# Weight steps handed out one at a time, token tiles as the outer loop of the second product, and sums of x made earlier

## The chip, the core and the metric

The kernel runs on one core of a Trainium2 chip. The metric is the device time of one execution in microseconds (us), the median of several runs. The engines are TensorE (PE in the profile; PEld is its weight load), VectorE (DVE), ScalarE (ACT), GpSimd (POOL) and the sync engine (SP), which only issues DMAs here. Each engine works through its own queue in order and waits on semaphores for the others.

## The reference

Three layers follow each other on 2 x 576 = 1152 tokens of width 512; all inputs are float32.

```python
# 1. attention with a window of 128 and a bias that falls with distance, 8 heads of 64
scores = where(mask, scale * q @ k.T + bias, -1e9)
x = softmax(scores) @ v
# 2. four experts, mixed by given weights p (rows of domain_probs, normalised)
for e in range(4):
    h = maximum(x @ w1[e], 0)            # 512 -> 1024
    out += p[:, e:e+1] * (h @ w2[e])     # 1024 -> 512
# 3. squared relu
h = maximum(out @ w_in, 0)               # 512 -> 2048
return (h * h) @ w_out                   # 2048 -> 512
```

## The kernel before, in words

Precision: each float32 operand is split into a rounded high part and a low part (`wh` and `wl`, `xh` and `xl`, `hh` and `hl`), and each product is three matmuls: high by high, high by low, low by high. ScalarE makes the high part by a copy, VectorE or GpSimd the low part by a subtraction.

Attention, with 24 of the 32 items of expert 0 between it, is ordered by a planner (class `Plan`), which the change does not touch. What follows is written out by a loop over `items`. An item is one piece of the first product of a layer: for expert 0 and for the last layer (which counts as experts 4 and 5) it is one slice of 128 hidden units on a chunk of 256 or 384 tokens (`gemm1`, 12 matmuls). For experts 1 to 3 it is a pair: `gemm1_pair` computes 256 hidden units for two blocks of tokens (2 x 256 in chunk 0, 2 x 320 in chunk 1) by seven products of 6 matmuls each instead of eight. It does so with sums and differences of the weights (`ha`, `hs` and low parts `la`, `ls`, made by `w_forms`) and of x (`t1`, `t2`, `m4`, `t3`, made by `x_forms`; the high part is `ht`, `hm` or is written into `xh` itself). In the order of the products: `p1` is ScalarE's copy of the first, `u2` VectorE's sum of the second with it, `p5` ScalarE's copy of the third; then relu of the first quarter, `u3`, `c12` with its relu, `c21` with its relu, and GpSimd's `c22` with its relu. Three PSUM banks take the seven products, and the second use of a bank waits until VectorE or ScalarE has read the first. TensorE therefore waits for `p1`, `u2`, `p5` and `u3` if they come late. The profile calls them `p`, `u` and `c`.

`pend` holds the h of one pair (or of three items of `gemm1`) back. `flush_one` then does the second product (`gemm2_pair` or `gemm2`, outputs `yacc`, one PSUM bank for each tile of 128 tokens) and, at the last slice, `evac` empties the banks into `y`. In a pair the loop over the two halves of h is the outer one and the loop over tiles the inner one, and `evac` comes after all tiles.

Weights: `loads` issues the DMA of a weight from the sync queue when a buffer is free. `w_ops` gives the list of steps that turn a loaded weight into its parts. For experts 1 to 3 that is one step for `w2` (ScalarE `wh`, 128 x 1024, then GpSimd `wl`) and ten for `w1` (ScalarE `ha`; four GpSimd sums `wsum`; two GpSimd `la`; ScalarE `hs`; GpSimd `ls`). For the last layer, whose weights come as 64-bit numbers, there are 14 steps on ScalarE and VectorE (`split64`, lines 199 to 214, with `wh` and `wl` at L326 and L328). The list `bg` holds the steps that are not yet issued. Once for each item `pace` computes a quota from the times at which the items should begin (`begins`), and `bg_some` issues half of it behind the first product and half behind the second. `want` issues what is still missing of the weight that comes next. `x_step` issues one of the six steps of `x_forms`, three times in an item that is a pair and once otherwise.

So it is the place in this loop that fixes where a step stands in the queue of its engine: behind an item's own instructions, in front of the next item's.

Of the kernel before, what the change touches and what calls it, by code (L numbers as in the profile page):

```python
# [130 lines left out]
def kernel(  # L131
# [132 lines left out]
    def w_forms(i):  # L264
# [27 lines left out]
        def done():  # L292
# [12 lines left out]
            lambda: (part_lo(4, 2, a22), free.append(buf)),  # L305
            lambda: nc.scalar.activation(out=t["hs"][0], in_=t["s"], func=ACTF.Copy),
# [573 lines left out]
    def gemm1_pair(e, ch, g):  # L880
# [36 lines left out]
        add(u2, pb, p1)  # L917
        mm(pc, s1, f["t1"], True, False)
        nc.scalar.activation(out=p5, in_=pc, func=ACTF.Copy)
        mm(pa, a12, f["b21"], False, True)  # L920
        relu(0, 0, pa)
        mm(pb, s3, f["t3"], False, False)
        add(u3, pb, p1)
        mm(pc, s4, f["b22"], False, True)
        add(c12, pc, u2)
        relu(0, 1, c12)
        mm(pb, a22, f["m4"], False, True)
# [3 lines left out]
        relu(1, 1, c22)  # L931
        return h

    def gemm2_pair(e, ch, g, h, tiles, first, last):
        (wh, _), (wl, _) = w2t[e, g]
        for fo, (hh, hl) in enumerate(h):
            for i, y in tiles:
                ns = slice(i * P, (i + 1) * P)
                for j, (l_, r_) in enumerate(((hh, wh), (hh, wl), (hl, wh))):
                    nc.tensor.matmul(  # L940
                        out=y, lhsT=l_[:, ns], rhs=r_[:, fo, :],
                        start=(first and fo == 0 and j == 0),
                        stop=(last and fo == FTQ - 1 and j == 2),
                    )
# [110 lines left out]
    def flush_one():  # L1055
# [8 lines left out]
        if paired(e):  # L1064
            gemm2_pair(e, ch, f, h, ys[e, ch], first, last)
        else:
            gemm2(e, ch, f, h, ys[e, ch])
        w_done(w2t, e, ch, f)
        if last:
            tiles = ys.pop((e, ch))  # L1070
            evac(e, ch, tiles)
            if e == E - 1 and f == NQ - 1:
                x2todo.extend(PAIRS[ch][0] // P + i for i, _ in tiles)
# [36 lines left out]

    def closures(i):
        e, _, k = order[i]
        return 14 if e >= E else 10 if paired(e) and k == 0 else 1

    def pace(it):
# [3 lines left out]
        for i in range(wnext["ops"], min(wnext["ops"] + 12, len(order))):  # L1119
            n += closures(i)  # L1120
            most = max(most, n / max(begins[item_of(i)] - 6.0 - now, step))
        return -int(-most * step // 1)
# [199 lines left out]
    xbg = x_forms(0, "DVE") + [[]] * 2 + x_forms(1, "DVE")  # L1322
# [20 lines left out]
    for it, (e, ch, f) in list(enumerate(items))[N1:]:  # L1343
# [7 lines left out]
        quota = pace(it)  # L1351
# [18 lines left out]
        x_step()  # L1370
# [50 lines left out]
```

## Time and profile before

| | us |
|---|---|
| median of 3 runs | 710.21 |
| the runs | 708.23, 710.21, 710.31 |
| profiled execution | 708.31 |
| its span, first to last instruction | 706.5 |
| TensorE matmul busy | 677.6 (96%) |
| VectorE busy | 413.3 (58%) |
| ScalarE busy | 298.6 (42%) |
| GpSimd busy | 295.9 (42%) |

The busy share of TensorE is that of records whose ends are modelled, so it does not say that the array is at its peak; it says where TensorE had nothing to run. [...] Times in rows are counted from the start of the span. Attention and the planner's items end at about 153, expert 0 at about 185, experts 1 to 3 at about 497, and the last layer takes the rest.

### The profile page before, as it was taken

Reading aid. Unit: us, or ns where it says so; the run is one execution under the profiler, and the core shown is the slowest. Engines: PE = TensorE matmul, PEld = TensorE weight load, DVE = VectorE, ACT = ScalarE, POOL = GpSimd, SP = SyncE. Lnnn points to the kernel's source line nnn. Section 1 sums busy time; section 2 is a strip of 40 time slices with the busy share of each in tenths; the row PEclk is TensorE's granted clock in tenths of the full one; section 3 lists DMA queues with packets and bytes.
Section 4 is the critical chain, followed back from the end, with each engine's and each line's share of the span. In section 5 each row is a group of like instructions: output and inputs, shape, how many; then the busy total and the mean of one; then the engine's idle time right before and its main releaser. Section 6 shows DMA issues by size and latency. Waiting matters only on the chain.

```text
span 706.5 us, 10701 instructions
## 1 busy us (share of the span) xinstructions
PE 677.6 (96%) x3992; PEld 610.4 (86%) x3992; DVE 413.3 (58%) x880; ACT 298.6 (42%) x700; POOL 295.9 (42%) x314
## 2 busy tenths in 40 slices
PE   8789999999969999999998999989989999999997
PEld 7689999899957989898988999887979999989996
DVE  4778787639287454445442546876886676542121
ACT  5977676624133342333333234333445444432221
POOL 4998656535243664734836351000222223222221
PEclk7989999999979999999999999999999999999999
DMA  8752221003101100101101102216520120001011
GB/s 216 221 145 79 73 79 51 10 31 120 59 31 57 63 31 31 60 32 59 60 31 61 60 0 90 90 60 221 196 61 0 60 90 30 2 1 45 1 45 45
DMA packets 37108, 47.63 MB, mean 67 GB/s; under 512 B 3392, under 2 KB 25408, under 8 KB 37056
## 3 DMA queue, kind: packets, MB, share of 16 engines
q1 hardware_dynamic: 37056, 46.95, 20.9%
q8 instruction: 31, 0.51, 0.3%
q14 instruction: 21, 0.17, 0.1%
HBM read 44.58 MB, written 2.36 MB: 66 GB/s over the span
## 4 chain that ended last, share of the span: by engine, by line
PE 87%; DVE 6%; ACT 2%; POOL 2%; issue 1%; SPq 1%; DMA 1%; ACTq 0%; POOLq 0%
PE yacc L940 20%; PE yacc L971 20%; PE hps L810 20%; PE hps L891 18%; PE xps L631 4%; PE tp L733 2%; PE sc L685 2%; DVE fxwork L846 1%; DVE wl L328 1%; DMA wraw<-in_w_dram 1%; SPq L1164 1%; POOL wl L402 1%; DVE wroom L214 1%; ACT wh L326 0%; PE xps L613 0%
## 5 line engine op out<-in xcount | busy, mean ns | idle before, releaser
L971 PE MATMUL yacc<-wh,hmem 128*128 128x512 f32 x432 | 147.5, 394 | 0.0
L940 PE MATMUL yacc<-wh,hmem 128*128 128x512 f32 x432 | 137.1, 390 | 0.0
L961 POOL TENSOR_TENSOR hmem<-r,hmem 128x384 fp32r<-128x384 f32 x48 | 52.1, 1085 | 167.2 <-ACT hmem L960 167.2
L810 PE MATMUL hps<-xh,wh 128*128 128x384 f32 (+1 forms) x320 | 104.0, 325 | 1.6 <-ACT wh L326 1.3
L810 PE MATMUL hps<-xh,wl 128*128 128x384 f32 (+1 forms) x320 | 102.8, 321 | 0.6 <-DVE wl L328 0.6
L810 PE MATMUL hps<-xl,wh 128*128 128x384 f32 (+1 forms) x320 | 102.3, 320 | 0.0
L940 PEld LDWEIGHTS yacc<-wh,hmem 128*128 128x128 f32 x432 | 81.1, 188 | 16.4
L971 PEld LDWEIGHTS yacc<-wh,hmem 128*128 128x128 f32 x432 | 81.2, 188 | 15.3
L971 PE MATMUL yacc<-wl,hmem 128*128 128x512 f32 x216 | 85.1, 394 | 0.0
L940 PE MATMUL yacc<-wl,hmem 128*128 128x512 f32 x216 | 84.3, 390 | 0.0
L930 POOL TENSOR_TENSOR c<-u,p 128x256 f32<-128x256 f32 (+1 forms) x24 | 19.5, 814 | 144.3 <-DVE u L901 144.3
L959 DVE TENSOR_TENSOR r<-hps,r 128x384 f32<-128x384 f32 x48 | 26.7, 556 | 79.0 <-ACT r L958 79.0
L810 PEld LDWEIGHTS hps<-xh,wh 128*128 128x128 f32 x320 | 60.3, 189 | 4.9 <-ACT wh L326 1.7
L810 PEld LDWEIGHTS hps<-xl,wh 128*128 128x128 f32 x320 | 60.3, 188 | 2.3
L958 ACT ACTIVATE r<-hps 128x384 f32<-128x384 f32 x48 | 23.5, 490 | 90.0 <-PE hps L810 90.0
L810 PEld LDWEIGHTS hps<-xh,wl 128*128 128x128 f32 x320 | 60.2, 188 | 1.2 <-DVE wl L328 1.2
L905 ACT ACTIVATE hmem<-c 128x256 fp32r<-128x256 f32 (+1 forms) x72 | 29.4, 439 | 74.1 <-DVE c L901 74.1
L906 DVE SCALAR_TENSOR_TENSOR hmem<-c,hmem 128x256 fp32r<-128x256 f32 (+1 forms) x72 | 45.7, 661 | 24.5 <-ACT hmem L905 24.5
L901 DVE TENSOR_TENSOR u<-hps,p 128x256 f32<-128x256 f32 (+1 forms) x48 | 21.8, 455 | 58.0 <-PE hps L891 49.2
L721 POOL TENSOR_SCALAR ts<-ts,st 128x256 f32<-128x256 f32 (+2 forms) x80 | 38.4, 495 | 28.1 <-DVE st L716 14.4
L940 PEld LDWEIGHTS yacc<-wl,hmem 128*128 128x128 f32 x216 | 40.6, 188 | 7.7
L971 PEld LDWEIGHTS yacc<-wl,hmem 128*128 128x128 f32 x216 | 40.6, 188 | 6.5
(130 smaller groups left out, 1550.3 us busy)
## 6 DMA issues: line engine op xcount, KB each, us to landing
wraw<-in_w_dram SPq DMA_DIRECT2D x32, 512.0 KB, 3.5
wraw<-in_w_in_dram SPq DMA_DIRECT2D x16, 512.0 KB, 4.3
wraw<-in_w_out_dram SPq DMA_DIRECT2D x16, 512.0 KB, 3.6
rq<-in_qT_dram SPq DMA_DIRECT2D x8, 256.0 KB, 5.9
out_dram<-y SPq DMA_DIRECT2D x8, 256.0 KB, 2.1
rk<-in_kT_dram SPq DMA_DIRECT2D x8, 192.0 KB, 3.5
rv<-in_v_dram SPq DMA_DIRECT2D x8, 192.0 KB, 2.9
rq<-in_qT_dram SPq DMA_DIRECT2D x8, 192.0 KB, 2.5
```

The costliest lines, as they stand in the source:

```text
L631: nc.tensor.matmul(out=xps[0:rows, o0:o0 + w], lhsT=l_, rhs=r_, start=start, stop=(i == len(mm) - 1 and a == 0 and l_ is wl_), skip_group_ ...
L721: nc.gpsimd.tensor_scalar(out=ts[0:n, g, :], in0=ts[0:n, g, :], scalar1=st[0:n, 2, g:g + 1], scalar2=1.0, op0=ALU.mult, op1=ALU.mult,)
L810: nc.tensor.matmul(out=ps, lhsT=l_[:, k, cs], rhs=r_[:, k, cols], start=(k == 0 and r_ is xh and l_ is wh and not second), stop=(k == KT - ...
L891: nc.tensor.matmul(out=ps, lhsT=a[l_][:, k, :], rhs=b[r_][:, k, :], start=start and k == 0 and l_ == r_, stop=stop and k == 1 and l_ == 1, ...
L901: nc.vector.tensor_tensor(out=out, in0=x, in1=y, op=ALU.add)
L905: nc.scalar.activation(out=hh, in_=src, func=ACTF.Relu)
L906: nc.vector.scalar_tensor_tensor(out=hl, in0=src, scalar=0.0, in1=f32(hh), op0=ALU.max, op1=ALU.subtract)
L940: nc.tensor.matmul(out=y, lhsT=l_[:, ns], rhs=r_[:, fo, :], start=(first and fo == 0 and j == 0), stop=(last and fo == FTQ - 1 and j == 2),)
L958: nc.scalar.activation(out=r, in_=ps, func=ACTF.Relu)
L959: nc.vector.tensor_tensor(out=r, in0=ps, in1=r, op=ALU.mult)
L961: nc.gpsimd.tensor_tensor(out=hl, in0=r, in1=f32(hh), op=ALU.subtract)
L971: nc.tensor.matmul(out=y, lhsT=l_[:, ns], rhs=r_[:, fo, :], start=(f == 0 and j == 0), stop=(f == FT - 1 and j == 2),)
```

## The change

1. `fill(share)` is new. It adds a share of the item's quota to an account and issues a step for each whole one. `gemm1_pair` calls it behind five of its seven products, and `flush_one` behind each tile of a second product. The two calls of `bg_some` for each item are gone. `pace` returns a number that is not rounded, and it wants the weights of a pair 12 us ahead instead of 6.
2. The list of steps of `w_forms` gets two empty steps ahead of `hs`.
3. `gemm2_pair` does one tile for both halves of h before the next one, and `evac` of a tile follows that tile.
4. The steps of `x_forms` for chunk 1 follow those of chunk 0 without a gap, two in an item, so that they are all issued within expert 0, the last two behind its last item.
5. `loads` is called a second time in each item.

```diff
--- before.py
+++ after.py
@@ -303,6 +303,8 @@
             lambda: add(6, lambda: a12, s(2), ALU.subtract),
             lambda: part_lo(0, 4, raw[:, :, 0:P]),
             lambda: (part_lo(4, 2, a22), free.append(buf)),
+            lambda: None,
+            lambda: None,
             lambda: nc.scalar.activation(out=t["hs"][0], in_=t["s"], func=ACTF.Copy),
             done,
         ]
@@ -915,33 +917,38 @@
         nc.scalar.activation(out=p1, in_=pa, func=ACTF.Copy)
         mm(pb, s2, f["t2"], True, False)
         add(u2, pb, p1)
+        fill(0.6)
         mm(pc, s1, f["t1"], True, False)
         nc.scalar.activation(out=p5, in_=pc, func=ACTF.Copy)
+        fill(0.6)
         mm(pa, a12, f["b21"], False, True)
         relu(0, 0, pa)
         mm(pb, s3, f["t3"], False, False)
         add(u3, pb, p1)
+        fill(0.6)
         mm(pc, s4, f["b22"], False, True)
         add(c12, pc, u2)
         relu(0, 1, c12)
+        fill(0.6)
         mm(pb, a22, f["m4"], False, True)
         add(c21, pb, p1)
         relu(1, 0, c21)
         nc.gpsimd.tensor_tensor(out=c22, in0=u3, in1=p5, op=ALU.add)
         relu(1, 1, c22)
+        fill(0.6)
         return h
 
-    def gemm2_pair(e, ch, g, h, tiles, first, last):
+    def gemm2_pair(e, ch, g, h, tile_, first, last):
         (wh, _), (wl, _) = w2t[e, g]
+        i, y = tile_
+        ns = slice(i * P, (i + 1) * P)
         for fo, (hh, hl) in enumerate(h):
-            for i, y in tiles:
-                ns = slice(i * P, (i + 1) * P)
-                for j, (l_, r_) in enumerate(((hh, wh), (hh, wl), (hl, wh))):
-                    nc.tensor.matmul(
-                        out=y, lhsT=l_[:, ns], rhs=r_[:, fo, :],
-                        start=(first and fo == 0 and j == 0),
-                        stop=(last and fo == FTQ - 1 and j == 2),
-                    )
+            for j, (l_, r_) in enumerate(((hh, wh), (hh, wl), (hl, wh))):
+                nc.tensor.matmul(
+                    out=y, lhsT=l_[:, ns], rhs=r_[:, fo, :],
+                    start=(first and fo == 0 and j == 0),
+                    stop=(last and fo == FTQ - 1 and j == 2),
+                )
 
     def gemm1(e, ch, f):
         n = chunks(e)[ch][1]
@@ -1061,14 +1068,17 @@
         if first:
             n = 2 * PAIRS[ch][1] if paired(e) else chunks(e)[ch][1]
             ys[e, ch] = [(i, ps_tile("y", [P, DM], "yacc")) for i in range(n // P)]
-        if paired(e):
-            gemm2_pair(e, ch, f, h, ys[e, ch], first, last)
-        else:
-            gemm2(e, ch, f, h, ys[e, ch])
+        for tile_ in ys[e, ch]:
+            if paired(e):
+                gemm2_pair(e, ch, f, h, tile_, first, last)
+            else:
+                gemm2(e, ch, f, h, [tile_])
+            if last:
+                evac(e, ch, [tile_])
+            fill(1.0)
         w_done(w2t, e, ch, f)
         if last:
             tiles = ys.pop((e, ch))
-            evac(e, ch, tiles)
             if e == E - 1 and f == NQ - 1:
                 x2todo.extend(PAIRS[ch][0] // P + i for i, _ in tiles)
 
@@ -1108,18 +1118,29 @@
                 w_start()
             bg_run(1)
 
+
+    quota = dict(n=0, per=1.0, left=0.0)
+
+    def fill(share):
+        quota["left"] += quota["n"] * share / quota["per"]
+        while quota["left"] >= 1.0:
+            quota["left"] -= 1.0
+            bg_some(1)
+
     def closures(i):
         e, _, k = order[i]
-        return 14 if e >= E else 10 if paired(e) and k == 0 else 1
+        return 14 if e >= E else 12 if paired(e) and k == 0 else 1
 
     def pace(it):
 
         n, most = len(bg), 0.0
         now, step = begins[it], begins[it + 1] - begins[it]
         for i in range(wnext["ops"], min(wnext["ops"] + 12, len(order))):
+            e = order[i][0]
             n += closures(i)
-            most = max(most, n / max(begins[item_of(i)] - 6.0 - now, step))
-        return -int(-most * step // 1)
+            early = 12.0 if paired(e) else 6.0
+            most = max(most, n / max(begins[item_of(i)] - early - now, step))
+        return most * step
 
     def w_done(parts, e, ch, f):
         if paired(e):
@@ -1319,7 +1340,7 @@
     attn_close()
     fxwork, fxbuf = zip(*(w_tile([P, 2 * PAIRS[1][1]], F32, "fxwork") for _ in range(2)))
 
-    xbg = x_forms(0, "DVE") + [[]] * 2 + x_forms(1, "DVE")
+    xbg = x_forms(0, "DVE") + x_forms(1, "DVE")
 
     def x_step():
         if xbg:
@@ -1348,7 +1369,7 @@
             want(2 * (pend[0][0] * NQ + (pend[0][2] if paired(pend[0][0]) else pend[0][2] // FTQ)) + 1)
         if it > x2wait and (it - x2wait) % 2:
             run_x2()
-        quota = pace(it)
+        quota["n"] = pace(it)
         if paired(e):
             h = gemm1_pair(e, ch, f)
             if it == items.index((E, 0, 0)) - 1:
@@ -1367,15 +1388,17 @@
                 flush_one()
         pend.append((e, ch, f, h))
         w_done(w1t, e, ch, f)
-        x_step()
+        loads()
+        for _ in range(2):
+            if e or len(xbg) > 2 or f == FT - 1:
+                x_step()
         if paired(e):
-            x_step()
-        bg_some(quota - quota // 2)
+            quota["per"] = 3.0 + 2 * PAIRS[ch][1] / P
+        else:
+            quota["per"] = 1.0 + chunks(e)[ch][1] / P
+            fill(1.0)
         if len(pend) > (1 if paired(e) else LAG):
             flush_one()
-        if paired(e):
-            x_step()
-        bg_some(quota // 2)
     while bg or carry:
         bg_run()
         while carry:
```

The order of instructions shows three places. In the names, `wraw` is a loaded weight, `fxwork` the room in which a sum of x is made, and `yacc` and `hps` are PSUM banks; a number behind a name tells apart what would read alike. The line numbers of the changed kernel differ from those of the kernel before by 2 to 7 here.

On ScalarE, from the last relu of the first pair to the second pair's copies `p`, about 191 to 207 in the profile. Before:

```order
L905 ACTIVATE hmem<-c_2542 128x256
L864 ACTIVATE ht_2636<-fxwork 128x640
L306 ACTIVATE hs<-wsum 128x1024
L326 ACTIVATE wh<-wraw 128x1024
L864 ACTIVATE ht_2642<-fxwork 128x640
L287 ACTIVATE ha<-wraw 128x512
L287 ACTIVATE ha<-wraw 128x256
L915 ACTIVATE p_2668<-hps 128x256
L919 ACTIVATE p_2669<-hps 128x256
```

The same place in the changed kernel:

```order
L907 ACTIVATE hmem<-c_2566 128x256
L287 ACTIVATE ha<-wraw 128x512
L287 ACTIVATE ha<-wraw 128x256
L308 ACTIVATE hs<-wsum 128x1024
L328 ACTIVATE wh<-wraw 128x1024
L917 ACTIVATE p_2689<-hps 128x256
L922 ACTIVATE p_2690<-hps 128x256
```

The two `ht` of chunk 1 (L864) are gone from between the pairs. `hs`, `wh` and one `ha` still stand ahead of the second pair's `p`.

On VectorE, the end of expert 0 up to the first `u` of the first pair, about 169 to 186 in the profile; L953 is the split of h of an item of expert 0. Before:

```order
L846 TENSOR_TENSOR lt_2331<-fxwork,ht_2330 128x512
L846 TENSOR_TENSOR fxwork<-xh 128x512
L846 TENSOR_TENSOR fxwork<-fxwork,xl 128x512 x2
L953 SCALAR_TENSOR_TENSOR hmem<-hps,hmem 128x384
L846 TENSOR_TENSOR lm_2361<-fxwork,hm_2360 128x512
L953 SCALAR_TENSOR_TENSOR hmem<-hps,hmem 128x384
L846 TENSOR_TENSOR xl<-fxwork,xh 128x2x256
L953 SCALAR_TENSOR_TENSOR hmem<-hps,hmem 128x384 x2
L901 TENSOR_TENSOR u_2538<-hps,p_2536 128x256
```

The same place in the changed kernel (L960 is the split):

```order
L848 TENSOR_TENSOR fxwork<-xh,fxwork 128x640
L848 TENSOR_TENSOR fxwork<-fxwork,xl 128x640
L848 TENSOR_TENSOR lt_2409<-fxwork,ht_2408 128x640
L848 TENSOR_TENSOR fxwork<-xh 128x640
L848 TENSOR_TENSOR fxwork<-fxwork,xl 128x640 x2
L960 SCALAR_TENSOR_TENSOR hmem<-hps,hmem 128x384 x3
L848 TENSOR_TENSOR lm_2446<-fxwork,hm_2445 128x640
L848 TENSOR_TENSOR xl<-fxwork,xh 128x2x320
L903 TENSOR_TENSOR u_2562<-hps,p_2560 128x256
```

The work of chunk 1 (640 columns) has moved in ahead of the last three splits of expert 0, and its last two instructions stand ahead of the first `u`.

On VectorE, from the emptying of five tiles in expert 3 to the next pair's `u`, about 441 to 450 in the profile. Before:

```order
L328 TENSOR_TENSOR wl<-wroom,wh 128x512
L214 SCALAR_TENSOR_TENSOR wroom<-wroom 128x512
L203 TENSOR_SCALAR wroom<-wraw_4783 128x512
L989 SCALAR_TENSOR_TENSOR y<-yacc,pt,y 128x512 x5
L206 TENSOR_SCALAR wroom<-wroom 128x512
L210 SCALAR_TENSOR_TENSOR wroom<-wraw_4783,wroom 128x512
L328 TENSOR_TENSOR wl<-wroom,wh 128x512
L214 SCALAR_TENSOR_TENSOR wroom<-wroom 128x512
L203 TENSOR_SCALAR wroom<-wraw_4903 128x512
L901 TENSOR_TENSOR u_4911<-hps,p_4909 128x256
```

The same place in the changed kernel:

```order
L996 SCALAR_TENSOR_TENSOR y<-yacc,pt,y 128x512
L210 SCALAR_TENSOR_TENSOR wroom<-wraw_4774,wroom 128x512
L330 TENSOR_TENSOR wl<-wroom,wh 128x512
L214 SCALAR_TENSOR_TENSOR wroom<-wroom 128x512
L996 SCALAR_TENSOR_TENSOR y<-yacc,pt,y 128x512 x2
L203 TENSOR_SCALAR wroom<-wraw_4776 128x512
L206 TENSOR_SCALAR wroom<-wroom 128x512
L996 SCALAR_TENSOR_TENSOR y<-yacc,pt,y 128x512
L210 SCALAR_TENSOR_TENSOR wroom<-wraw_4776,wroom 128x512
L330 TENSOR_TENSOR wl<-wroom,wh 128x512
L903 TENSOR_TENSOR u_4908<-hps,p_4906 128x256
```

The five emptyings (L989, now L996) no longer stand in one piece: steps of the last layer's weights stand between them, and two instead of five stand between the last of them and `u`.

## Rows read from the trace of the kernel before

**Rows 1.** Busy time by stretch: stretch; its length; PE, PEld, DVE, ACT, POOL; clock; DMA

```profile
184.70:211.20 26.50, 19.90 (x113) 17.98 (x112) 17.34 (x23) 7.73 (x16) 8.62 (x6) 0.81 0.09 32
204.00:211.20 7.20, 6.95 (x35) 6.65 (x36) 5.21 (x6) 1.08 (x3) 5.12 (x5) 0.61 0.21 73
475.70:479.30 3.60, 3.60 (x16) 3.60 (x15) 1.21 (x3) 0.47 (x1) 0.86 (x1) 0.53 0.02 5
540.00:700.00 160.00, 160.00 (x800) 144.34 (x799) 71.02 (x116) 58.31 (x113) 40.48 (x38) 1.00 0.09 30
```

**Rows 2.** Waits of TensorE: who waited for whom; us in total, times, longest

```profile
PE hps L891 <- ACT hs L306: 4.3, 1, 4.3
PE hps L891 <- ACT p L915: 3.6, 2, 1.8
PE hps L891 <- DVE u L901: 3.3, 2, 1.9
```

**Rows 3.** The chain that ended last: start, us, what

```profile
184.88 5.12 PE hps L891 x42
...
211.17 5.47 PE yacc L940 x24
...
219.57 1.04 ACT hs L306
...
220.99 3.78 PE hps L891 x24
...
265.74 6.15 PE hps L891 x42
...
466.68 0.34 DVE wroom L203
...
467.36 0.60 DVE wroom L210
```

**Rows 4.** Timeline, VectorE and ScalarE, 194 to 201: start, us, instruction, [idle before <-releaser]

```profile
194.82 2.11 DVE L985 TENSOR_SCALAR y<-yacc,pt 128x512 f32<-128x512 f32 x3 [2.69 <-PE yacc L971]
...
199.41 0.74 ACT L864 ACTIVATE ht<-fxwork 128x640 fp32r<-128x640 f32 x1 [7.76 <-DVE fxwork L846]
200.06 1.04 ACT L306 ACTIVATE hs<-wsum 128x1024 fp32r<-128x1024 f32 x1
```

**Rows 5.** Timeline around three later waits of TensorE, 386 to 476

```profile
386.28 1.06 ACT L306 ACTIVATE hs<-wsum 128x1024 fp32r<-128x1024 f32 x1 [4.78 <-POOL wsum L281]
...
387.24 1.04 ACT L326 ACTIVATE wh<-wraw 128x1024 fp32r<-128x1024 f32 x1
...
388.61 0.38 PE L891 MATMUL hps<-xh,ha 128*128 128x256 f32 x1 [1.84 <-ACT p L915]
...
443.84 3.38 DVE L989 SCALAR_TENSOR_TENSOR y<-yacc,pt,y 128x512 f32<-128x512 f32 x5
...
450.08 0.39 PE L891 MATMUL hps<-xh,hs 128*128 128x256 f32 x1 [1.42 <-DVE u L901]
...
475.06 0.41 PE L891 MATMUL hps<-xh,hs 128*128 128x320 f32 x1 [1.91 <-DVE u L901]
```

**Rows 6.** Sums of x: line L846 in one stretch, then VectorE and GpSimd beside them

```profile
156.00:184.70 28.70, 16.01 (x14) 1.00 0.30 100
...
156.25 0.56 DVE L953 SCALAR_TENSOR_TENSOR hmem<-hps,hmem 128x384 fp32r<-128x384 f32 x1 [3.23 <-ACT hmem L952]
...
163.61 0.68 DVE L846 TENSOR_TENSOR lt<-fxwork,ht 128x512 fp32r<-128x512 f32 x1
...
164.65 2.64 POOL L402 TENSOR_TENSOR ls<-wsum,hs 128x1024 fp32r<-128x1024 f32 x1 [4.44 <-ACT hs L306]
...
165.05 2.78 DVE L846 TENSOR_TENSOR fxwork<-fxwork,xl 128x512 f32<-128x512 f32 x1
...
386.20 1.97 POOL L402 TENSOR_TENSOR la<-wraw,ha 128x512 fp32r<-128x512 f32 x2
...
388.12 2.39 POOL L402 TENSOR_TENSOR ls<-wsum,hs 128x1024 fp32r<-128x1024 f32 x1
```

## The prediction

> **What bounds the kernel now.** I read the profile in this order: the granted clock and busy time by stretch, the waits of TensorE, the chain that ended last, then the timeline around each wait. [...]
>
> Undisturbed, a pair product (42 matmuls) takes 5.12 us at 256 tokens and 6.15 us at 320, so one of its seven products takes 0.73 or 0.88 us; a second product of 24 matmuls takes 5.47, or 0.228 each [rows 3].
>
> **Term A, expert 0 to expert 1.** From 184.88 to 211.17 TensorE does two pairs and 27 matmuls of `yacc` [rows 3]: 2 x 5.12 + 27 x 0.228 = 16.4 us of work in 26.3 us. The loss is 9.9 us. The cause stands in the timeline [rows 4]: VectorE empties three `y` tiles (2.11 us from 194.82) and then makes chunk 1's sums of x. ScalarE's `ht` waits 7.76 us for them, and behind it in ScalarE's queue stands `hs`, which TensorE needs. [...]
>
> The change takes these sums out of that stretch: the order of ScalarE shows no `ht` ahead of `hs` there any more. But VectorE must now do them in the items before. Its queue from the split at 156.25 [rows 6] to the last split of expert 0 holds 14 instructions of 512 columns at 0.68, 12 of 640 columns (at 0.68 x 640/512 = 0.85 by proportion, an estimate), 8 splits of 0.5 (0.56 [rows 6] less the overlap of one with the next) and 2 emptyings at 0.70 (a third of 2.11 [rows 4]): 9.5 + 10.2 + 4.0 + 1.4 = 25.1 us. To this come the times in which GpSimd holds VectorE up. The rows show the hold-up: at 165.05 a 0.68 us instruction took 2.78 us, and ended as GpSimd's `ls`, begun at 164.65 for 2.64 us, was over; the 14 instructions took 16.0 instead of 9.5 us, 6.5 more [rows 6]. Laid out in the new order, one after the other, the collisions that I find are the last weight sum (0.6), about 0.8 of the pair of `la` (1.97), 1.4 of the first `ls` (2.39 less a split that reads PSUM beside it) and all of one `wl` (the size of `ls`, 2.39): 5.2 us. VectorE also idles some 1.2 us for ScalarE's copies. That puts the last split at 156.25 + 25.1 + 5.2 + 1.2 = 187.8, and the third last, which frees the PSUM bank that the first pair begins in, about 1.0 us earlier: 186.8. TensorE wants the bank at 184.88: a wait of 1.9 us that was not there before. Bounds: no collisions give 181.6 and no wait; the 6.5 us of before, again in proportion for the 12 (5.6), give 193.7 and a wait of 8.8. I take 1.9, the layout by single rows.
>
> [...]
>
> Behind the wait two small ones follow. In the first pair `u` stands behind the last two forms (2 x 0.85), which take turns with four GpSimd sums: I get 1.3 us (bounds 0 and 3). In the second pair `p` stands behind `hs` and `wh` (1.06 and 1.04 [rows 5]), and `hs` waits for GpSimd's sums, which queue behind `ls` and `wl`: 1.5 us (bounds 0 and 3). [...] New loss 1.9 + 1.3 + 1.5 + 0.8 = 5.5; gain 9.9 - 5.5 = **4.4**.
>
> **Term B, the third pair.** `p` came late behind `hs` at 219.57 [rows 3], which waited for the last forms. The two waits for `p` sum to 3.6 us, the longest is 1.8 [rows 2]; this one is the other, 1.7, and the restart costs 3.78 - 24 x 0.146 = 0.3. With no form and no step of weights in ScalarE's queue there any more, **2.0** are gained; bounds 0 and 2.0.
>
> **Term C, the pair at 388.** `hs` waited 4.78 us for GpSimd's sums, `wh` came behind it, and `p` behind both; TensorE lost 1.84 [rows 5]. The two empty steps put `hs` later than the sums, and `fill` puts it between tiles of a second product. Gain **1.8**; bounds 0 and 2.1.
>
> **Term D, the pair at 450.** Five emptyings (3.38 us) stood in a lump with the steps ahead of `u`; TensorE lost 1.42 [rows 5]. Now each tile is emptied as it is finished, but the count of steps is the same. After the preceding pair VectorE has its tail (three instructions and the copies between them, 2.4 us by estimate), 5 x 0.68 of emptying (3.38 / 5 [rows 5]) and nine step instructions (four at 0.34 and five at 0.60 [rows 3]: 4.4): 10.2 us against 30 matmuls, 30 x 0.228 = 6.8. `u` then starts 3.4 - 0.2 us into a pair that asks for it after 4 x 0.73 = 2.9 and needs 0.4 for it: 0.6 stays. Gain **0.8**; bounds -1 and 1.4.
>
> **Term E, the pair at 475.** [...] By the reckoning of D: 2.4 + 4 x 0.68 + 2.5 = 7.6 us against 5.47, so `u` is done 2.6 us into a pair that asks for it at 4 x 0.88 = 3.5. Gain 1.9 + 1.3 = **3.2**; bounds 0 and 3.2.
>
> **Term F, steps within the pairs.** 18 of the 24 pairs now get one to seven steps between their products. Costly is the place after the third product: `p` has been copied, and ScalarE's relu of the first quarter follows, from which `h`'s low part and then `u`'s successor hang, due 1.46 (256) or 1.76 us (320) later. The chain itself needs about 1.3 or 1.65, so a ScalarE step of 1.04 there shows as some 0.3 us. In the new order such a step (`wh`, or the first of a squared-relu weight) stands there in four pairs; elsewhere it is a GpSimd step, an empty one, or stands after the critical instruction. Loss 4 x 0.25 = **1.0**; bounds 0 and, if all 18 pay 1 us, 18.
>
> **Edits at nothing.** The tile-outer order changes neither the number nor the shape of matmuls, and each tile's six follow each other as twelve already do in the first product; what hides the later release of the second weights is that they are let go once per item, as before. Earlier `loads()` moves DMAs on the sync queue ahead; no wait of TensorE's after 150 is on one. Waits of the squared-relu layer's first items (`wh` and `wl`, about 2 us) stay: the step they hang on is still given out just ahead; bounds -2 and +2. In the last 180 us nothing waits, so finer hand-outs gain nothing.
>
> **Sum.** 4.4 + 2.0 + 1.8 + 0.8 + 3.2 - 1.0 = 11.2 us. The profiled execution took 708.31 (span 706.5 and 1.8 around it): 697.1. The median of the runs shown is 710.21, 1.9 above it, the other runs at 708.23 and 710.31; I say **697.5**, a little above the sum.
>
> **Rivals.**
> 1. The forms overload VectorE: every collision counts, the first pair waits 8.8 instead of 1.9 us and the clock falls as before (2.9 instead of 0.8). For it: 16.0 us for 9.5 us of work. Against it: of the 28.7 us of that row the 14 instructions, the splits and the emptyings leave 28.7 - 16.0 - 4.0 - 1.4 = 7.3 free. Time 697.1 + 6.9 + 2.1 = 706.1. Chance 0.12.
> 2. The lumps near the last expert only change shape, since VectorE's total there is the same: D and E stay, 697.1 + 4.0 = 701.1. Chance 0.13.
> 3. The spread steps cover everything: the new waits of A and F and the rest of D vanish, 697.1 - 5.5 - 1.0 - 0.6 = 690.0. Chance 0.12.
> 4. Slower: steps within the pairs. A ScalarE step of 1.05 us with a VectorE step of up to 0.69 behind it in front of the accumulating quarter holds TensorE in each of the 18 pairs. It undoes the gain from (11.2 + 1.0) / 18 = 0.68 us a pair on; at 0.9 a pair, 697.1 - 1.0 + 16.2 = 712.3. For it: before, no pair had steps inside, and its slack is 0.1 to 0.2 us. Against it: most steps there are GpSimd's. Chance 0.08.
>
> My forecast, 693 to 702, has 0.55. The range 689.5 to 705.5 holds the forecast, rivals 2 and 3 and part of the first. A measurement of this kernel can tell about 0.3% (2.1 us) from no change. Faster than that: forecast, rivals 2 and 3 and most of 1, 0.87; slower 0.08; between them 0.05.
>
> **What would show it.** [...] The prediction is wrong if the first pair waits over 6 us, if the pairs show TensorE waiting in most of them, or if the last 180 us change.

## The result and the profile after

The changed kernel takes 700.83 us (median of 4 runs, 700.31 to 702.1) against 709.91 us: 0.9879 of the time before, with a 95% interval of 0.9857 to 0.9901. Timed once more in a later comparison it came to 0.9863 (0.9842 to 0.9885). The forecast was 697.5 with a range of 689.5 to 705.5: right in sign and range, 3.3 us too low. How far its reasons held is told term by term further down.

TensorE's waits from the trace after answer to [rows 2] (who waited for whom; us in total, times, longest):

```profile
PE hps L893 <- ACT p L917: 1.8, 1, 1.8
PE hps L893 <- DVE u L903: 1.8, 3, 0.7
PE xtp L1009 <- DVE xl L1014: 1.5, 1, 1.5
PE xtp L1009 <- DVE c L903: 1.4, 1, 1.4
...
PE hps L812 <- ACT wh L328: 1.1, 1, 1.1
PE hps L812 <- DVE wl L330: 1.0, 1, 1.0
...
PE hps L893 <- DVE hmem L960: 0.7, 1, 0.7
```

The kernel before also had these, which [rows 2] leaves out:

```profile
PE hps L891 <- POOL ls L402: 2.2, 1, 2.2
PE hps L810 <- ACT wh L326: 1.3, 1, 1.3
PE xtp L1002 <- DVE xl L1007: 1.0, 1, 1.0
PE hps L810 <- DVE wl L328: 0.6, 1, 0.6
```

The 4.3 us for `hs` and the 2.2 for `ls` are gone. The 3.6 for `p` have become one wait of 1.8, and the 3.3 for `u` three waits of at most 0.7. The transposes (`xtp`) of the last layer's input, which waited once for 1.0 us, now wait twice, 2.9 us together. The waits for `wh` and `wl` in the last layer have stayed at some 2 us.

The chain of work that ended last answers to [rows 3] (start, us, what):

```profile
182.86 2.87 POOL wl L330
...
190.85 2.48 PE hps L893 x18
193.33 6.15 PE yacc L978 x27
199.48 2.16 PE hps L893 x18
...
202.07 1.04 ACT wh L328
203.11 0.28 ACT p L917
...
203.43 4.31 PE hps L893 x24
207.74 5.81 PE yacc L947 x24
```

The 24 second-product matmuls of the first pair start at 207.74; before, they started at 211.17 [rows 3]. In front of them stands what is left of the loss: `p` came late because ScalarE still had `wh`, and `hs` ahead of that, to do. The trace shows ScalarE doing them in the order of its queue: `p` follows at 203.11, at the end of the 1.04 us of `wh`, though its matmuls were done at 201.64.

Busy time by stretch answers to [rows 1] (columns as there; the clock is the granted TensorE clock as a share of its full speed):

```profile
183.00:213.00 30.00, 26.77 (x150) 23.54 (x149) 18.05 (x26) 11.40 (x24) 25.39 (x19) 0.94 0.20 70
203.40:207.80 4.40, 4.37 (x25) 4.37 (x26) 2.02 (x5) 1.05 (x3) 4.40 (x3) 0.67 0.27 89
512.30:513.30 1.00, 0.94 (x3) 0.95 (x4) 1.00 (x4) 0.36 (x1) 0.00 (x0) 0.50 0.42 94
553.00:613.00 60.00, 60.00 (x302) 54.28 (x301) 36.70 (x60) 26.90 (x52) 16.13 (x14) 1.00 0.11 36
```

Two stretches run below full clock: 203.4 to 207.8 (0.67) and a little beyond (0.87 up to 210.0), behind the wait for `p`, and 512.3 to 515.6 (0.51), behind the waits for `wh` and `wl`. After that the squared-relu layers run as before, with no idle time: TensorE is busy for all of the 60.00 us of the last row, at 1.00.

The timeline answers to [rows 4] and [rows 5] (start, us, instruction, [idle before <-releaser]):

```profile
174.44 0.74 ACT L866 ACTIVATE ht<-fxwork 128x640 fp32r<-128x640 f32 x1 [4.89 <-DVE fxwork L848]
...
182.63 3.77 DVE L848 TENSOR_TENSOR fxwork<-fxwork,xl 128x640 f32<-128x640 f32 x2
...
201.10 1.06 ACT L308 ACTIVATE hs<-wsum 128x1024 fp32r<-128x1024 f32 x1 [1.74 <-POOL wsum L281]
...
443.54 0.39 PE L893 MATMUL hps<-xh,hs 128*128 128x256 f32 x1 [0.72 <-DVE u L903]
...
473.74 0.44 PE L1009 MATMUL xtp<-ident,y 128*128 128x128 f32 x2 [1.54 <-DVE xl L1014]
```

`ht` now waits at 174, where TensorE has other work. The two sums at 182.63 take 3.77 us where two of them alone took 0.82 each just before: GpSimd's `wl` runs from 182.86 to 185.72 beside them. That is the hold-up of [rows 6] once more.

**Where the gain stands.** I take the start of the same second product in every trace: before, 182.63, 224.61, 377.62, 391.67, 464.01, 482.57 and 530.35; after, 183.97, 219.54, 373.39, 385.34, 457.46, 474.15 and 523.39. The same +1.34 of the first stands already at 102.92 against 104.26 us, far ahead of the change, so it is a difference between executions and is taken off. Gains over before in us, stretch by stretch, for the profiled execution of each kernel below; the last three columns are their sum, and the median and ratio of the timed runs. Each ratio is to the kernel before as timed beside it (708.3 to 709.9 us), so rows are better compared by ratio than by median:

| kernel | to 225 | to 378 | to 392 | to 464 | to 483 | to 530 | sum | median | ratio (95%) |
|---|---|---|---|---|---|---|---|---|---|
| changed | 6.4 | -0.8 | 2.1 | 0.2 | 1.9 | -1.5 | 8.3 | 700.8 | 0.9879 (0.9857-0.9901) |
| changed, again (e5) | 6.5 | -0.8 | 2.1 | 0.2 | 1.5 | -2.7 | 6.8 | 700.0 | 0.9863 (0.9842-0.9885) |
| e1 early sums alone | 9.3 | 0.0 | -1.4 | 0.0 | 1.0 | 0.0 | 8.8 | 699.4 | 0.9859 (0.9841-0.9878) |
| e2 sums as before | 2.4 | -1.4 | 2.1 | -0.3 | 1.5 | -2.5 | 1.8 | 706.3 | 0.9952 (0.9935-0.9969) |
| e3 none within pairs | 3.0 | 0.0 | 2.1 | -4.1 | 1.4 | -0.8 | 1.6 | 703.2 | 0.9937 (0.9911-0.9963) |
| e4 tiles inner | 7.7 | -0.8 | 2.1 | 0.2 | 1.9 | -1.4 | 9.7 | 700.7 | 0.9873 (0.9856-0.9890) |
| e6 shares add to one | 9.9 | -0.9 | 2.1 | 0.1 | 0.9 | -3.2 | 8.9 | 700.8 | 0.9866 (0.9841-0.9892) |
| e7 + none in last pair | 10.0 | -0.9 | 2.1 | 0.1 | 3.2 | -3.5 | 11.0 | 697.3 | 0.9825 (0.9801-0.9849) |
| e8 + last weights early | 9.9 | -0.9 | 2.1 | -0.7 | 3.1 | 3.1 | 16.5 | 692.8 | 0.9762 (0.9739-0.9785) |
| e9 lumps, due early | 7.1 | 0.0 | 2.1 | -0.6 | -0.9 | 2.4 | 10.1 | 699.8 | 0.9870 (0.9852-0.9888) |
| e10 changed, last early | 6.4 | -0.8 | 2.1 | 0.0 | 2.1 | -0.1 | 9.7 | 698.6 | 0.9861 (0.9844-0.9878) |
| e11 no empty steps | 6.1 | -1.0 | 2.1 | -1.2 | 1.9 | -1.7 | 6.2 | 703.0 | 0.9915 (0.9896-0.9934) |

### The profile page after: what moved, and what is told of

It is laid out like the page before. It is cut to its first block, busy times and chain, and to the rows that moved or that the text cites. A ratio compares the mean times of both kernels' runs of the same rounds, so it can differ in the third digit from the quotient of the medians.

```text
span 699.5 us, 10689 instructions
## 1 busy us (share of the span) xinstructions
PE 678.3 (97%) x3992; PEld 611.6 (87%) x3992; DVE 412.2 (59%) x880; ACT 297.7 (43%) x700; POOL 294.8 (42%) x314
## 4 chain that ended last, share of the span: by engine, by line
PE 84%; DVE 8%; ACT 3%; issue 2%; POOL 1%; DMA 1%; SPq 1%; ACTq 0%; DVEq 0%; POOLq 0%
PE yacc L947 20%; PE hps L812 19%; PE yacc L978 19%; PE hps L893 17%; PE xps L633 4%; PE tp L735 2%; PE sc L687 2%; DVE fxwork L848 1%; DMA wraw<-in_w_dram 1%; SPq L1185 1%; POOL ts L723 1%; DVE wl L330 1%; DVE st L715 0%; PE xps L615 0%; DVE wroom L210 0%
## 5 line engine op out<-in xcount | busy, mean ns | idle before, releaser
L908 DVE SCALAR_TENSOR_TENSOR hmem<-c,hmem 128x256 fp32r<-128x256 f32 (+1 forms) x72 | 49.5, 712 | 26.7 <-ACT hmem L907 26.7
L936 POOL TENSOR_TENSOR c<-u,p 128x256 f32<-128x256 f32 (+1 forms) x24 | 21.4, 892 | 104.0 <-DVE u L903 104.0
L723 POOL TENSOR_SCALAR ts<-ts,st 128x256 f32<-128x256 f32 (+2 forms) x80 | 40.0, 513 | 28.6 <-DVE st L718 15.5
```

The source lines that it names most:

```text
L723: nc.gpsimd.tensor_scalar(out=ts[0:n, g, :], in0=ts[0:n, g, :], scalar1=st[0:n, 2, g:g + 1], scalar2=1.0, op0=ALU.mult, op1=ALU.mult,)
L908: nc.vector.scalar_tensor_tensor(out=hl, in0=src, scalar=0.0, in1=f32(hh), op0=ALU.max, op1=ALU.subtract)
```

## The experiments

**e1: the early sums alone**, in the kernel before.

```
-    xbg = x_forms(0, "DVE") + [[]] * 2 + x_forms(1, "DVE")
+    xbg = x_forms(0, "DVE") + x_forms(1, "DVE")
-        x_step()
-        if paired(e):
-            x_step()
+        for _ in range(2):
+            if e or len(xbg) > 2 or f == FT - 1:
+                x_step()
...
-        if paired(e):
-            x_step()
```

> The kernel before with one part of the change alone: the second chunk's sums of x are issued within the first expert's last chunk (no two empty steps, two steps an item). The weights' steps stay in two lumps an item. Theory (the earlier sums are what takes away the waits for hs and ls at 201 and 204 us): between the last split of the first expert and the end of the third pair the kernel gains 5 to 6.4 us, and nothing behind 225 us changes: the waits at 388 (1.8), 450 (1.4) and 475 us (1.9 and the clock) stay. Time 703.5 to 705 against 709.9, ratio about 0.992. Rival (overload: VectorE and GpSimd are full there, so the sums only move the wait, and it is the spread weights' steps that gain): at most 2 us, 708 to 710, with a wait of 3 us or more in the first or second pair.

Measured: 699.37 us, as fast as the whole change (0.9859 against 0.9879 and 0.9863). Theory and rival both fell short. The sums bring 9.3 us up to 225, not 6.4, and the rest of the change, as written, adds nothing on top. TensorE's waits in this trace:

```profile
PE hps L891 <- DVE u L901: 3.3, 2, 1.9
PE hps L891 <- DVE hmem L953: 2.3, 1, 2.3
PE hps L891 <- ACT p L915: 1.8, 1, 1.8
...
PE xtp L1002 <- DVE c L901: 0.7, 1, 0.7
```

The 2.3 us is the wait for the freed bank that term A put at 1.9. Nothing stands behind it: no `p`, no `u`, no low clock. The waits for `u` and `p` are the later ones, untouched as expected; the last row is taken up below. Its busy time by stretch:

```profile
183.00:213.00 30.00, 27.74 (x171) 24.98 (x170) 16.54 (x29) 10.72 (x22) 14.06 (x12) 1.00 0.16 53
379.00:382.00 3.00, 3.00 (x18) 3.00 (x19) 1.16 (x3) 0.52 (x2) 3.00 (x2) 0.65 0.03 10
466.00:472.00 6.00, 4.43 (x30) 3.95 (x30) 3.70 (x10) 1.65 (x4) 0.88 (x1) 1.00 0.24 81
```

TensorE is busy 27.74 of the 30 us, against 26.77 in the changed kernel, and GpSimd 14.06 against 25.39. The second row is the -1.4 of the table: behind the wait for `p` at 379 (1.83 us) the clock fell, and in the kernel before, behind 1.84 us in the same place [rows 5], it did not:

```profile
183.00:213.00 30.00, 23.40 (x129) 20.81 (x128) 19.08 (x27) 8.77 (x19) 10.42 (x8) 0.83 0.12 41
389.00:392.00 3.00, 3.00 (x25) 2.93 (x25) 1.22 (x5) 0.80 (x2) 3.00 (x2) 1.00 0.14 25
```

The third row of e1 is the 1.0 that it gains up to 483, and there it is the other way round. The wait for `u` is 1.91 us in both kernels (at 466.81 here, at 475.06 before); before, the clock fell behind it ([rows 1], 0.53), and here it held at 1.00. That is worth 1.7 us: the 1.0 gained, and 0.7 that is lost again, since at full clock TensorE reaches the transposes before `c` is there. In the kernel before no such wait shows; the low clock had hidden it.

**e2: the changed kernel with the sums back in their old place** (the lines of e1 undone).

> The changed kernel with the sums of x put back to where they were (two empty steps between the chunks, three steps a pair); everything else as changed. Theory: hs and ls come late again, waits of about 4.3 and 2.1 us at 200 to 205 us with the clock at half behind them, 5 to 6.4 us lost there; the gains at 388, 450 and 475 us stay. Time about 706 to 707, ratio to the kernel before about 0.995. This version's list of steps has also no lump of weights' steps ahead of the last layer's seventh product, so that the waits of 1.1 and 1.0 us for wh and wl at 510 us and the half clock behind them should go (3 us or so): then 703.5 to 704.5. Rival (the spread weights' steps alone bring hs early enough): the waits at 200 us are under 1.5 us, time 698 to 701.

Measured: 706.33 us, within the theory's first figure; the second, with the half clock at 510 gone, was wrong: the waits for `wh` and `wl` (1.1 and 1.0) stood there still, so the lump of steps was not their cause. TensorE waited in one piece at the handover:

```profile
204.66 0.58 PE L893 MATMUL hps<-xh,ha 128*128 128x256 f32 x1 [6.45 <-ACT p L917]
```

So the spread steps without the early sums bring 2.4 us up to 225 and some 3 us in all (the medians differ by 2.7, the ratio gives 3.4); with the 9.7 of e1 the two parts come to more than the 9.1 of the whole.

**e3: no steps within pairs**, all five places of `fill` in `gemm1_pair` taken out.

```
-        fill(0.6)
...
-            quota["per"] = 3.0 + 2 * PAIRS[ch][1] / P
+            quota["per"] = 2 * PAIRS[ch][1] / P
```

> The changed kernel without steps between the seven products of a pair; their share goes to the tiles of the second product. Theory (steps within pairs cost some 0.4 us in two pairs at 263 and 311 us, 0.3 at 432 and 0.7 at 443): these four waits go, 1.5 to 2 us, and the two waits of transposes at 471 and 474 us shorten; the order of steps here has also no lump ahead of the last layer's seventh product, worth about 3 us. Time 695.5 to 698.5. Rival 1 (steps within pairs are nearly free and what they keep apart is the lumps between tiles): the waits at 388, 450 and 475 us come back at 1.4 to 2 us each, time 701 to 705. Rival 2 (steps cost in every pair, 0.3 us or more): all 18 pairs get shorter, 5 us or more gained outside the places named.

Measured: 703.23 us. Six of its ten runs took 701.7 to 703.5 us and four 707.3 to 708.7; the profiled one (707.31) is one of the four, so its row in the table overstates the loss. The small waits at 263 and 311 went (0.0 in the second column), so term F is real and small, 0.8 us. In the changed kernel's trace the step stands where F put it, ahead of ScalarE's relu of the first quarter:

```profile
263.72 1.05 ACT L328 ACTIVATE wh<-wraw 128x1024 fp32r<-128x1024 f32 x1
264.67 0.43 ACT L907 ACTIVATE hmem<-hps 128x320 fp32r<-128x320 f32 x1
```

But the steps, pushed together between tiles, came back as larger waits elsewhere, as rival 1 said in kind: the wait at 388 that it named did not come, and the longest came where it had named none:

```profile
PE hps L893 <- ACT p L917: 5.6, 2, 4.6
...
PE hps L893 <- DVE u L903: 3.6, 3, 1.7
```

The 4.6 stood at 205; at 444 and 447 a wait for `p` (1.05) and one for `u` (1.65) followed each other, and at 474 one for `u` of 1.2. Rival 2 is out: apart from the pairs at 263, 311 and 432, none got shorter.

**e4: tiles the inner loop again** in the pairs, `y` emptied behind the last tile.

```
-    def gemm2_pair(e, ch, g, h, tile_, first, last):
+    def gemm2_pair(e, ch, g, h, tiles, first, last):
         for fo, (hh, hl) in enumerate(h):
+            for i, y in tiles:
                 ...
+                fill(1.0 / FTQ)
...
+            gemm2_pair(e, ch, f, h, ys[e, ch], first, last)
+            if last:
+                evac(e, ch, ys[e, ch])
```

> The changed kernel with the second product of the pairs in the order of before: tiles the inner loop, the rounding of all tiles (y) behind the last of them; the steps keep their number, half a share behind each tile of either half. Theory (the tile order is worth nothing by itself): 700.8 within 1.0, the waits of the trace at the same places. Rival (tile by tile the y results leave VectorE early, and that is what took the waits at 450 and 475 us away): those waits come back at 1.4 and 1.9 us with half a clock behind the second, time 703 to 705.

Measured: 700.71 us, the same ratio, the waits in the same places with the same lengths. The order of the loops is worth nothing. Its 7.7 up to 225 instead of 6.4 is the clock: after the wait for `p` (1.82 us) it stayed at full.

```profile
202.40:206.80 4.40, 4.32 (x30) 4.08 (x31) 2.56 (x5) 1.11 (x4) 4.40 (x3) 1.00 0.29 97
```

**e5: the changed kernel again**, beside the next three.

> The changed kernel itself once more, beside the three that follow. Every theory: 0.9879 of the kernel before, within 0.002. In its trace the waits stand at the same places (0.7, 0.7 and 1.8 us between 186 and 204; 1.4 and 1.5 at the transposes; 1.1 and 1.0 in the last layer); what is open is whether the half clock behind the 1.8 us (1.3 us lost in the first trace) comes each time: if it comes by the wait alone, it is there again, if by chance it is there in some traces only.

Measured: 0.9863. The waits stand where they stood. The low clock behind the wait for `p` came again, and in e10 and e11 too (1.80, 1.79 us): granted 0.67, 0.61, 0.63 and 0.61 in four traces, 1.00 in e4. Here it fell at the transposes too, where in the first trace, behind the same waits, it had held:

```profile
471.10:474.50 3.40, 3.06 (x10) 2.58 (x11) 2.76 (x7) 2.20 (x5) 0.00 (x0) 0.50 0.37 141
```

That is 1.2 of the 2.7 us that its row loses up to 530.

**e6: shares that add up to one.** The changed kernel's hand-out has a slip. `quota["per"]` is set at an item's end for the next one, by the size of one second product. The first pair has three of them before it: its quota of 7.3 steps is divided by the 4 shares of the item ahead, and given out over 3 shares in the pair and 9 tiles, 7.3 x 12 / 4 = 22 steps. The first items of the squared-relu layer have no second product, and give out a quarter of their quota.

```
+        cold = bool(pend) and paired(e) != paired(pend[0][0])
+        due = pend if cold else pend[:1] if len(pend) + 1 > (1 if paired(e) else LAG) else []
+        quota["per"] = (3.0 if paired(e) else 1.0) + sum(n_tiles(p[0], p[1]) for p in due)
...
-            quota["per"] = 3.0 + 2 * PAIRS[ch][1] / P
-            quota["per"] = 1.0 + chunks(e)[ch][1] / P
```

> The changed kernel with the shares of a product's steps made to add up to one: in the changed kernel the item with three second products at the boundary of experts gives its quota out more than three times (some 22 steps where 7 are asked for), and the first items of the last layer, which have no second product, give out a quarter of theirs. Theory (the steps given out too many at the boundary cost what the earlier sums gain by themselves more than the whole change: 9.3 us against 6.4 up to the third pair's end): the waits for p (1.8) and u (0.7) at 190 to 204 us go, a wait for the bank of 2 us or so stays, and the stretch gains 8.5 to 9.3; the 2.1 us at 388 stay; the half clock at 513 us (1.4 us lost) goes or stays with the waits of 1.1 and 1.0 there. Time 696.5 to 698.5. Rival (any step in this stretch costs, GpSimd being busy 24 of 31 us, however it is given out): 700 to 702, with p or u still waited for there.

Measured: 700.8 us, the rival's figure, but not for its reason: `p` is not waited for (`u` is, 0.7 us), and the handover gains 9.9, more than in e1:

```profile
183.00:213.00 30.00, 28.56 (x172) 25.53 (x172) 17.21 (x27) 11.29 (x24) 23.03 (x18) 1.00 0.22 70
```

TensorE is busy 28.56 us, with GpSimd still at 23.03 (25.39 in the changed kernel). What held `p` there was not GpSimd's load as such, but the number of steps put ahead of `p` on ScalarE: two rounds of `hs` and `wh`, at 189.81 and again at 201.10, where `hs` waited 1.74 us for GpSimd's sums. Here ScalarE does one round between the pairs, and nothing in it is waited for:

```profile
195.20 1.05 ACT L308 ACTIVATE hs<-wsum 128x1024 fp32r<-128x1024 f32 x1
```

What was won there was lost behind the transposes (waits of 2.1 and 1.5 us, and a granted clock of 0.50 from 472 to 476) and in the last layer (0.4, 1.7 and 0.9 us for `wl`, `wh` and `wl`, 0.8 more than before). In the last layer the clock held:

```profile
509.00:520.00 11.00, 8.12 (x38) 6.82 (x39) 7.39 (x14) 4.32 (x9) 2.18 (x2) 1.00 0.30 96
```

**e7: and no steps within the last pair**, the one ahead of the transposes.

```
+        n_now, last_pair = quota["n"], it == items.index((E, 0, 0)) - 1
+        quota["n"] = 0.0 if last_pair else n_now
+        quota["per"] = (0.0 if last_pair else 3.0 if paired(e) else 1.0) + sum(n_tiles(p[0], p[1]) for p in due)
...
+        quota["n"] = n_now
         pend.append((e, ch, f, h))
```

> The same, and no steps between the products of the last pair, whose share goes to the tiles of the second product behind it. Theory (steps that stand ahead of c and xl on VectorE and of xh on ScalarE make the transposes wait 1.4 and 1.5 us where before only 0.7 and 1.0): these come down to 0.7 and 1.0 or less, 1 to 1.5 us less than the kernel with the shares alone: 695.5 to 697.5. Rival (the transposes wait for their own bank and its emptying): under 0.4 us.

Measured: 697.32 us, 0.9825. The transposes wait 0.7 and 1.0 us, as the theory said, and the stretch gains 3.2, which is what term E had promised. Without that edit 1.3 of it is thrown away: in the changed kernel's trace VectorE does `wl` (0.68 us at 467.93) and a step of L214 (0.68 at 469.96) among the last pair's `c`, and ScalarE a step of L199 (0.66 at 471.82) ahead of `xh`. In the trace of e7 the last layer's waits, and the low clock behind them, cost most of what is left to gain:

```profile
505.00:512.00 7.00, 5.52 (x15) 4.42 (x16) 4.99 (x8) 2.62 (x6) 1.73 (x2) 0.59 0.23 77
```

**e8: and the last layers' weights due 12 us ahead**, as the experts' are, in place of 6.

```
-            early = 12.0 if paired(e) else 6.0
+            early = 12.0 if e else 6.0
```

> The same, and the last layers' weights due 12 us ahead of their product in place of 6, as the experts' are. Theory (the fourth group of the last layer's weights has its last steps just ahead of its product in every version so far, which is why 2 us of waits for wh and wl stood at 503 to 521 us before and after alike): both waits go, and the clock behind them, 2 to 3.4 us less than the kernel ahead: 693 to 695. Rival (VectorE has no room for them in the last pairs): the waits for u come back at 430 to 475 us, 1.5 us or more each, and the time is the same or longer.

Measured: 692.83 us, the fastest here: 0.9762 (0.9739 to 0.9785) of the kernel before, and 7.2 us below the changed kernel beside it (e5, 700.04). Both waits are gone, and the clock holds:

```profile
505.00:512.00 7.00, 7.00 (x36) 6.26 (x35) 5.07 (x9) 3.94 (x8) 2.05 (x2) 1.00 0.16 56
```

TensorE's waits that are left after 150 us (the rival's waits for `u` came, but small):

```profile
PE hps L893 <- DVE u L903: 2.3, 3, 0.8
...
PE xtp L1009 <- DVE xl L1014: 1.0, 1, 1.0
PE hps L893 <- DVE hmem L960: 0.8, 1, 0.8
PE xtp L1009 <- DVE c L903: 0.7, 1, 0.7
```

**e9: early sums and early steps, but in lumps**: e1 with `begins[item_of(i)] - (12.0 if order[i][0] else 6.0)` in `pace`.

> The kernel before with the early sums of the first experiment and one number more: all the weights' steps of the experts and the last layers due 12 us ahead in place of 6 (the steps stay in two lumps an item, two outer loops of the second product as before). Theory (early sums and early steps carry the gain, giving steps out one at a time carries little): the early sums' 9.3 us stay, the waits for wh and wl of 2 us at 510 go, those at 380 (1.8), 442 (1.4), 467 (1.9) stay or shorten: 694.5 to 697.5. Rival (the even spread is what makes room for early steps, and without it they collide in the last pairs): 699 to 702, the waits at 440 to 470 grow by what is saved at 510.

Measured: 699.79 us, the rival's figure. The waits at 379 and 510 went (the third and the sixth column), and those of the last pairs grew, from 1.42 and 1.91 us to:

```profile
441.02 0.39 PE L891 MATMUL hps<-xh,hs 128*128 128x256 f32 x1 [2.02 <-DVE u L901]
...
466.95 0.41 PE L891 MATMUL hps<-xh,hs 128*128 128x320 f32 x1 [2.83 <-DVE u L901]
```

The handover gains 7.1 instead of the 9.3 of e1, since the clock fell behind the wait for the bank (2.5 us; from 188.1 to 191.3 the matmuls of 256 columns start 0.21 us apart, where they stand 0.12 apart just before, and the granted clock over 183 to 213 is 0.94). Against e8 the kernel is 7 us slower: giving steps out one at a time, with right shares, none in the last pair and the two empty steps, is worth that much, two falls of the clock in this trace (there and at 467.8, 0.66 over 467 to 472) included. Which of these carries how much was not tried from this side, nor was the second call of `loads` tried alone.

**e10: the changed kernel with e8's line alone.**

> The changed kernel with one number changed: the last layers' weights due 12 us ahead of their product in place of 6; the shares and the steps in the last pair stay as changed. Theory (the waits for wh and wl at 510 us and the clock behind them are the lateness of these steps alone): 2.2 us of waits and 1.3 us of clock go, 696.5 to 698. Rival (without right shares and with steps in the last pair the earlier steps go where the transposes wait): these grow past 3 us with half a clock behind, 699 to 701.

Measured: 698.6 us, 0.9861 (0.9844 to 0.9878), not to be told from the changed kernel's two ratios. The waits for `wh` and `wl` fell from 1.1 and 1.0 to 0.5 each. Part of the rival came true as well: behind the second wait of the transposes (1.6 us) the clock fell, as it had not in the first trace of the changed kernel, and took some 1.3 us back (up to 530 the waits are 1.2 us shorter than before, and the column shows -0.1):

```profile
473.40:476.00 2.60, 2.56 (x9) 2.15 (x10) 2.38 (x4) 1.68 (x3) 0.00 (x0) 0.60 0.57 217
```

**e11: the changed kernel without the two empty steps** (`closures` counts 10 steps again).

> The changed kernel without the two empty steps between the last GpSimd step of a weight's sums and the rounding of hs. Theory (they hold hs back from the front of ScalarE's queue in the pair at 380 us, where before p waited 1.8 us behind wh): the wait for p comes back there at 1 us or more, or elsewhere, 1 to 2 us slower: 701.5 to 703. Rival (the even spread alone has taken that wait away): 700 to 701, no wait at 380 to 390 us.

Measured: 702.98 us, 0.9915 (0.9896 to 0.9934). The wait for `p` at 388 did not come back (2.1 gained there as ever), so the empty steps are not what takes it away. Nor is the hand-out needed for it: e9, which has lumps and no empty steps, gains the same 2.1 there, and differs from e1, which has the wait, only in the due time of 12 us. Yet the kernel of e11 is slower, by new waits for `u`:

```profile
337.75 0.39 PE L891 MATMUL hps<-hm,ha 128*128 128x256 f32 x1 [0.39 <-DVE u L901]
...
396.41 0.39 PE L891 MATMUL hps<-xh,hs 128*128 128x256 f32 x1 [0.85 <-DVE u L901]
```

These lie at other places than the theory named. Whether the empty steps themselves or the shifted phase of all later steps does it stays open.

## Why the prediction was right, and where not

**A and B, the handover: the sum right, its inside wrong.** 6.4 forecast, 6.4 and 6.5 measured. Of the new loss the bank wait was 0.7 (forecast 1.9), `u` 0.7 (1.3), `p` 1.8 (1.5); the low clock behind it cost 4.31 - 24 x 0.122 = 1.4 on the pair's last four products and 5.81 - 5.47 = 0.3 on the next 24 matmuls (0.8 forecast for the clock in all). These errors, and a gain without them of some 11.3 where A and B took 11.9, cancel to 0.1 us; that is luck. No run shows the 0.8 that the sum has for the clock; the trace has the 1.4 and 0.3 in its place. `u` and `p` came about as described, `u` behind the last two sums of x and `p` behind `hs` and `wh`. The step of the reasoning that failed is that `p` was booked as a price that the gain of the early sums has to pay. e1 shows that the sums cost a bank wait of 2.3 us and no more, and e6 that bank and `u` together cost 1.4; they gain 9 to 10 us. `p` and the clock behind it are the price of 22 steps where 7 were asked for. I had read the two empty steps and the places of `fill` in the order, but not counted how many steps the first pair's item holds.

**C** was right in size, 2.1 for 1.8, its upper bound, and wrong in its cause. Neither the empty steps (e11) nor the hand-out (e9) is needed; the due time of 12 us takes the wait away by itself (e9 against e1), and the prediction did not book it anywhere. Whether it alone does so in the changed kernel was not tried.

**D** was right: 0.7 of waiting left where 0.6 was forecast, with `u` behind VectorE's steps as described. The table shows only 0.2 there, because a wait of F (0.3 at 432) falls into the same stretch. **F** was right in size and in its cause, 0.8 us up to 378 and 0.3 at 432 for 1.0, though in three pairs, with 0.4 or 0.3 each.

**E was mis-sized: 1.9 for 3.2.** The wait for `u` went as said, and the low clock behind it with it (1.00 from 466 to 478). For the 1.3 that the sum counts for this clock, the trace before has 16 matmuls in 3.6 us at 0.53 [rows 1], where 16 x 0.146 = 2.3 would do; e1, where the clock held, shows 1.7 in its place. The step that failed is the silence about what the same pair does next: the transposes behind it hang on `c` and `xl`, and steps within the pair delayed both. They wait 1.4 and 1.5 us; without those steps (e7) 0.7 and 1.0, and the 3.2 are there. Even that figure is made up otherwise than forecast: the clock alone brings 1.0 (e1), since 0.7 of its 1.7 goes to the wait for `c`, and taking the wait for `u` away brings 2.2 more (e7 against e1).

**The edits at nothing.** The tile order is worth nothing (e4). The waits for `wh` and `wl` stayed, 2.2 us, as forecast, inside bounds of 2 either way; what I left out is that the clock may fall behind them, which made the -1.5 up to 530 in the first trace and as much of the -2.7 in the second. Of the ten traces with about these waits the clock fell behind them in six (0.51 from 512.3 to 515.6 in the changed kernel, 0.59 over 505 to 512 in e7) and held in four (before, at 1.00 over 515 to 525, e1, e3 and e6, at 1.00 over 509 to 520).

The sum: 11.2 forecast, less 1.3 in E and 1.5 behind `wh` and `wl`, is 8.4; the trace shows 8.3. The smaller errors of C, D and F cancel.

**The rivals.** Overload (1) did not come: the first pair waited 0.7 us, not 8.8. The 2.9 us that it counts for the clock are those of the trace before, 35 matmuls in 7.2 us at 0.61 [rows 1], where 35 x 0.122 = 4.3 would do; the changed kernel lost 1.7 (1.4 and 0.3). D and E staying (2) did not come. Full cover (3), at 690.0, was neared in e8 only, by two corrections and an earlier due time. Steps within pairs (4) cost 0.06 us a pair over 18, against the 0.68 from which they decide. No rival said what e1 shows: that one part of the change alone brings all of its gain, and the other parts, as written, cancel out.

## What to carry to other kernels

When work is handed out in shares, add up the shares item by item at the irregular places (the first and last item of a phase, an item with three of something or none): an even rate that is wrong there costs what it gains elsewhere. Try each part of a change alone before crediting it: here one part gave 9.7 us and the rest nothing on top of it, and the rest was worth some 7 us once it was put right and the last layers' weights were due earlier. After taking a stall away, follow the same engine's queue to the next consumer (here from `u` to the transposes) before booking the whole of it.

## What the runs showed of the hardware that I had not expected

In these traces the length of a short wait does not settle whether TensorE's granted clock falls after it. In the same place of the program 1.84 us of waiting left it at 1.00 (before) and 1.83 us brought it to 0.65 over 3 us (e1); in another, 1.91 us brought it to 0.53 (before) and left it at 1.00 (e1); behind `p` at the handover 1.79 to 1.82 us brought it to 0.61 to 0.67 in four traces and left it at 1.00 in one. What does settle it stays open. That alone moved these runs by 1.3 to 1.7 us each time, so a difference of this size between two single traces says nothing about the kernels.

GpSimd's load beside TensorE's critical pairs did not by itself hold TensorE up here: it was busy 23.0 us of 30 in e6 with TensorE at 28.6, against 25.4 and 26.8 in the changed kernel.
